# A list schedule's numbers, a port it now counts, and evictions over two chunks

## The chip, the cores and the metric

The kernel runs on one core of a Trainium2 chip: TensorE (PE, with its weight loads PEld), VectorE (DVE), ScalarE (ACT), GpSimd (POOL) and the DMA queue of SyncE (SP). The metric is the device time of one execution in microseconds, smaller is better. Before the change: median 906.44 us of 3 runs (905.68 to 906.60).

## The reference, cut to what matters

Windowed attention (4 batches, 8 heads, 576 positions, head size 64, each query sees itself and 63 keys before it), then two MLPs on the 2304 tokens of width 512, each with 2048 hidden units:

```python
scores = np.where(mask, scale * np.matmul(q, k.transpose(0, 1, 3, 2)), -1000000000.0)
attn = np.exp(scores - np.max(scores, axis=-1, keepdims=True))
attn = attn / (np.sum(attn, axis=-1, keepdims=True) + 1e-09)
x = np.matmul(attn, v)          # then laid out as 2304 tokens x 512
h = x @ w_in;  x = np.maximum(0.01 * h, h) @ w_out      # first MLP
h = x @ w_in2; out = (h * np.cos(h)) @ w_out2           # second MLP
```

## The kernel before, in words

**Arithmetic.** Matrix products of the MLPs are made in three passes: each operand is split into a high part and a low remainder (XH and XL for the activations, wh and wl for the weights, gh and gl for the hidden values), and high*high, high*low and low*high are summed in PSUM.

**Weights.** The host passes the weights as 64-bit words, 64 blocks of 512 KB. A block `u` goes through these operations: `wd` DMA into a staging tile `st`, `wv` and `ww` take the two 32-bit halves apart (ACT), `wb` three bit operations on DVE (L199, L200, L204: from `st` and `wa` to `wa` and `we`), `wm` and `wj` a product and a sum (L209, L213, POOL or DVE), `wh` rounds the high part (ACT), `wl` the remainder (L225, POOL or DVE).

**Attention.** 18 steps of 128 tokens. A step `i` has loads `lq`, `lv`; 32 score products `qk` (L278); per half of the heads `st` (mask L286 and row maximum L291, DVE), `ex` (4 exponentials, ACT), `re` (L303, L304, DVE), `no` (L308, POOL), `pt` (transposes L316, PE), `pe` (copy out of PSUM, L152 on ACT); then `pv` (32 products L328), `xh` (XH, ACT) and `xl` (XL, L337, DVE).

**MLPs.** Each layer is run in four phases of 4 chunks of 128 hidden units. In a phase the tokens go by in tiles; a chunk of a tile is a unit: `h` (12 products L420 to L422), `ca`, `mx`, `gh`, `gl` (split of the hidden values: ACT, DVE L430, ACT, DVE L435; in layer two a longer chain L458 to L468 and L442), and, two units behind, `o` (12 products L507 for 256 tokens) into accumulators `y`. After a tile's fourth chunk the accumulators are evicted: `ev`, L535 on DVE where a sum of earlier phases is added, a copy on ACT in a layer's first phase.

**What sets the order.** The first phase of layer one (9 tiles of 256 tokens, 36 units) runs together with the 18 attention steps and the first 16 weight blocks. Its order is made by `ListSchedule`: it places operations one by one, each on the engine where it would end first by a table of durations (`spared` is added for DVE where there is a choice), earliest due time (`s_due`, `w_due`, `u_due`) first among those that could start within `AT_ONCE`. What comes out is one fixed order for each engine; on the chip an engine runs its own list in that order and waits for data by semaphores only. After unit 38 a plain loop sets the order: `emit_H(i)`, `chain(i)`, `emit_O(i - 2)`, and then either all evictions that are waiting or, without any, pieces of weight work (`w_next`) and of the second layer's operand split (`x_next`). SP's DMAs are one queue in the order of the same list: a load that waits for a buffer holds those behind it.

Of the kernel before, what the change touches and what calls it, by code (L numbers as in the profile page):

```python
# [27 lines left out]
G = 4  # L28
# [3 lines left out]
TILES_FIRST = (256,) * 9  # L32
# [1 line left out]
TILES_LAST = (512, 512, 512, 512, 256)  # L34
T_SPLIT = 1536
SAME = dict(pe=0.0, dve=0.12, act=0.12, pool=0.05, dma=0.0, none=0.0)
AT_ONCE = 0.05
TILE_US, STEP_AHEAD = 18.0, 30.0
W_AHEAD, LATE_FROM, LATE_US = 22.0, 30.0, 8.0
SPARED_FIRST, SPARED = 0.3, 2.0  # L40
LAG = 2


class ListSchedule:
# [15 lines left out]
    def ready(self, name):  # L60
        ways, after, take, give, due, spared = self.ops[name]
        bufs = 0.0
        for x, p in enumerate(take):
            log, n = self.taken[p], self.pools[p] - take[:x].count(p)
            if len(log) >= n:
                t = self.given[p].get(log[-n])
                if t is None:
                    return None
                bufs = max(bufs, t + 0.2)
        if any(a not in self.done for a in after):  # L70
            return None
        best = None
        for engine, us, fn in ways:
            t = max(bufs, self.free.get(engine, 0.0))
            for a in after:
                t0, e0 = self.done[a]
                t = max(t, t0 + (SAME[engine] if e0 == engine else 0.35 if e0 == "pe" else 0.2))
            rank = t + us + (spared if engine == "dve" and len(ways) > 1 else 0.0)
            if best is None or rank < best[4]:
                best = (t, engine, us, fn, rank)  # L80
        return best

    def run(self):
        waiting = list(self.ops)
        while waiting:
            ready = [(name, r) for name in waiting if (r := self.ready(name)) is not None]
            assert ready, waiting[:40]
            now = min(r[0] for _, r in ready) + AT_ONCE
            name, (t, engine, us, fn, _) = min(
                (x for x in ready if x[1][0] <= now), key=lambda x: (self.ops[x[0]][4], x[1][0])  # L90
            )
            waiting.remove(name)
            take = self.ops[name][2]
            for x, p in enumerate(take):
                n = take[:x].count(p)
                self.taken[p].append((name, n) if n else name)
            fn(engine)
            end = self.free[engine] = t + us
            self.done[name] = (end + (1.1 if engine == "dma" else 0.0), engine)
            for p, taker in self.ops[name][3]:  # L100
                self.given[p][taker] = end
# [3 lines left out]
def attention_two_mlps(ctx, tc, q, k, v, w_in1, w_out1, w_in2, w_out2, out, seq):  # L105
# [164 lines left out]
    def a_scores(i, pool, tag):  # L270

        for hd in range(2):
            qk_t[i, hd] = pool.tile([P, NPR, P], F32, tag=tag, name=f"qk{i}_{hd}")
            S_t[i, hd] = sp.tile([P, NPR, P], F32, tag="S", name=f"S{i}_{hd}")
        for pr in range(NPR):
            for x in range(2):
                for hd in range(2):
                    nc.tensor.matmul(  # L278
                        qk_t[i, hd][halves[x], pr, :], qT[i][halves[hd], pr, halves[x]],
                        kT[i][halves[hd], pr, x * BLK:x * BLK + P], start=True, stop=True,  # L280
                    )
# [19 lines left out]
    def a_recip(i, heads):  # L301
        sums, inv = (sm_t[i][:, x, heads[0]:heads[-1] + 1, :] for x in (1, 2))
        nc.vector.tensor_scalar(out=inv, in0=sums, scalar1=1e-9, scalar2=None, op0=ALU.add)  # L303
        nc.vector.reciprocal(out=inv, in_=inv)  # L304
# [81 lines left out]
    work = []  # L386
# [12 lines left out]
    N = len(work)  # L399
    e_todo, x_todo = [], []  # L400

    def e_next(n, engine="act"):
        for _ in range(n):
            if e_todo:
                evac(*e_todo.pop(0), engine)
# [113 lines left out]
    def evac(w, d, y, engine="act"):  # L519
        l, p, t0, n = w["l"], w["p"], w["t0"], w["n"]  # L520
        if w["packed"]:
            b = t0 // P
            part, b = (YF[0], b) if t0 < T_SPLIT else (YF[1], b - T_SPLIT // P)
            dst = part[:, b:b + n // P, d:d + 2, :].rearrange("p b d t -> p d b t")
            y = y.rearrange("p (d b t) -> p d b t", d=2, t=P)
        elif l == 0:
            dst = yrange(t0, n, d)
            y = y.rearrange("p (b t) -> p b t", t=P)
        else:
            dst = yblock(t0 // P + d).rearrange("p k e -> p (k e)")  # L530
        sign = 1.0 if l == 0 else -1.0
        if p == 0:
            scaled(engine, dst, y, sign)
        else:
            nc.vector.tensor_tensor(out=dst, in0=dst, in1=y, op=ALU.add if l == 0 else ALU.subtract)  # L535
        if w["lastphase"]:
            if l == 0:
                x_todo.append((dst, d, t0, n))
            else:
                r0 = t0 + d * P  # L540
                nc.sync.dma_start(out=out[r0:r0 + P, :], in_=dst)
# [28 lines left out]
    n0 = len(TILES_FIRST) * G  # L570
# [8 lines left out]
            before[w_after[u]] = u  # L579

    def w_due(x):
        return x * TILE_US / 8 - W_AHEAD if x < 2 * G else LATE_FROM + LATE_US * (x - 2 * G)

    def add_w_dma(x):
        u = w_list[x]
# [6 lines left out]
    def ways(fn, **us):  # L592
        return [(e, t, fn) for e, t in us.items()]
# [14 lines left out]
        op("wl", ways(lambda e: w_lo(u, e), pool=1.24, dve=0.7), [f"wh{u}"], [], [("wa", f"wv{u}")])  # L608

    def s_due(i):  # L610
        return TILE_US / 2 * i - STEP_AHEAD

    def add_loads(i):
        ls.add(f"lq{i}", [("dma", 2.2, lambda e: qk_load(i))], [f"qk{i - 2}"] if i >= 2 else [], due=s_due(i) - 6.0)
# [2 lines left out]
    def add_attention(i):  # L617
        pool, tag = (ps_y, "y") if i < LEAD else (ps_a, "a")
        pairs = [f"{i}_{hd}" for hd in range(2)]
        prev = [f"{i - 1}_{hd}" for hd in range(2)]  # L620

        def op(kind, w, after, take=(), give=(), hd=None):
            name = f"{i}" if hd is None else pairs[hd]
            before = f"{i - 1}" if hd is None else prev[1] if hd == 0 else pairs[0]
            after = list(after) + ([kind + before] if kind + before in ls.ops else [])
            ls.add(kind + name, w, after, take, give, due=s_due(i), spared=SPARED)

        op("qk", ways(lambda e: a_scores(i, pool, tag), pe=1.1), [f"lq{i}"], [tag, tag, "S", "S"])
        for hd in range(2):
            taker = f"qk{i}" if hd == 0 else (f"qk{i}", 1)  # L630
            op("st", ways(lambda e, hd=hd: a_mask(i, hd), dve=1.32), [f"qk{i}"], give=[(tag, taker)], hd=hd)
            op("ex", ways(lambda e, hd=hd: a_exp(i, hd), act=1.62), ["st" + pairs[hd]], hd=hd)
        if i < LEAD:
            for hd in range(2):
                ls.add("re" + pairs[hd], ways(lambda e, hd=hd: a_recip(i, [hd]), dve=0.3), ["ex" + pairs[hd]], due=s_due(i))
        else:
            ls.add(f"re{i}", ways(lambda e: a_recip(i, [0, 1]), dve=0.32), ["ex" + pairs[1]], due=s_due(i))
        for hd in range(2):
            taker = f"qk{i}" if hd == 0 else (f"qk{i}", 1)
            op("no", ways(lambda e, hd=hd: a_norm(i, hd, e), pool=1.05, dve=0.75),  # L640
               ["re" + pairs[hd] if i < LEAD else f"re{i}"], hd=hd)
            op("pt", ways(lambda e, hd=hd: a_transpose(i, hd), pe=0.5), ["no" + pairs[hd]], ["a"], [("S", taker)], hd=hd)
            op("pe", ways(lambda e, hd=hd: a_transposed(i, hd, e), act=0.5, dve=0.66), ["pt" + pairs[hd]],
               ["PT"], [("a", "pt" + pairs[hd])], hd=hd)
        op("pv", ways(lambda e: a_values(i), pe=1.2), ["pe" + p for p in pairs] + [f"lv{i}"], ["a"],
           [("PT", "pe" + p) for p in pairs])
        op("xh", ways(lambda e: a_out(i, 0, e), act=0.5, dve=0.66), [f"pv{i}"])
        op("xl", ways(lambda e: a_out(i, 1, e), dve=0.62), [f"xh{i}"], give=[("a", f"pv{i}")])

    def u_due(i):  # L650
        return TILE_US * work[i]["ti"] + TILE_US / G * (i % G) + (TILE_US * len(TILES_FIRST) if i >= n0 else 0.0)

    def add_unit(i):
        w = work[i]
# [54 lines left out]
    for x in range(4 * G):  # L709
        add_weights(x)  # L710
    for i in range(n0 + LAG):
        add_unit(i)
# [6 lines left out]

    for i in range(n0 + LAG, N + LAG):  # L720
        if i < N:
            w_until(2 * work[i]["m"])
            emit_H(i)
        chain(i)
        w_until(2 * work[i - LAG]["m"] + 1)
        emit_O(i - LAG)
        if e_todo:
            e_next(len(e_todo))
        else:
            x_next(2)  # L730
            for _ in range(2 if i < N and work[i]["n"] == 512 else 1):
                w_next()
# [46 lines left out]
```

## Time and profile before

| | us |
|---|---|
| runs, median of 3 (lowest, highest) | 906.44 (905.68, 906.60) |
| profiled execution, its own time | 906.46 |
| its span in the profile | 904.7 |
| PE busy in the span | 868.3 (96%) |
| DVE, ACT, POOL busy | 599.8, 488.7, 294.7 |

The span runs from the first instruction to the last; 1.8 us of the execution's own time lie around it. Matmuls are pipelined: a matmul's duration overlaps the next one's, so counts of matmuls are turned into time by the pieces of the chain, which do not overlap. A busy PE at a granted clock of 1.00 of its full 2.4 GHz and one at half of that look alike; the clock column tells them apart.

### The profile page before, as it was taken

What the parts mean: (1) busy time and instruction counts of PE and PEld (TensorE: products, weight loads), DVE (VectorE), ACT (ScalarE), POOL (GpSimd) and SP (SyncE); (2) the same over time, 40 slices, a digit from 0 to 9 for tenths busy, and PEclk for the clock granted to TensorE, in tenths of its full rate; (3) what the DMA queues carried; (4) which work ended last, traced back from release to release, by engine and by line L of the source; (5) the groups of instructions that cost most, each with busy time, mean ns of one, the idle gap of its engine ahead of it and who ended that gap; (6) DMA issues with size and microseconds to landing.
All of it is one profiled execution on the core that took longest, in us unless ns stands there. A gap on an engine that the chain in (4) does not pass through costs nothing.

```text
span 904.7 us, 14203 instructions
## 1 busy us (share of the span) xinstructions
PE 868.3 (96%) x5424; PEld 743.5 (82%) x5424; DVE 599.8 (66%) x963; ACT 488.7 (54%) x1101; POOL 294.7 (33%) x257
## 2 busy tenths in 40 slices
PE   4489999999999999999999999999999999999998
PEld 3389999987888888988888888888888888788886
DVE  6997556566565555454785677767777777865565
ACT  6578677665433333424444567666555655544443
POOL 4545122156332133332566243322333233220000
PEclk9599999999999999999999999999999999999999
DMA  8456334112111011111111011101111011001111
GB/s 293 150 176 205 109 128 135 48 71 71 47 46 47 24 48 47 47 47 46 47 48 47 13 58 47 47 24 47 48 47 46 24 47 47 24 0 47 47 47 70
DMA packets 29092, 60.16 MB, mean 66 GB/s; under 512 B 2464, under 2 KB 11680, under 8 KB 29024
## 3 DMA queue, kind: packets, MB, share of 16 engines
q1 hardware_dynamic: 29024, 59.25, 19.1%
q8 instruction: 42, 0.69, 0.3%
q14 instruction: 26, 0.21, 0.1%
HBM read 54.53 MB, written 4.72 MB: 65 GB/s over the span
## 4 chain that ended last, share of the span: by engine, by line
PE 86%; DVE 8%; ACT 2%; issue 2%; DMA 1%; SPq 0%; POOL 0%; ACTq 0%; DVEq 0%; POOLq 0%
PE y L507 40%; PE h L420 14%; PE h L421 14%; PE h L422 14%; PE pv L328 2%; DVE wa L200 1%; PE pt L316 1%; DVE wa L199 1%; PE qk L278 1%; DMA qT<-in_q_dram 1%; DVE S L286 1%; DVE we L204 1%; DMA st<-in_moe_w_in_dram 1%; DVE YFa L535 1%; DVE sm L291 0%
## 5 line engine op out<-in xcount | busy, mean ns | idle before, releaser
L420 PE MATMUL h<-XH,wh 128*128 128x512 f32 (+1 forms) x704 | 250.9, 356 | 3.2 <-DVE ca L442 3.2
L421 PE MATMUL h<-XL,wh 128*128 128x512 f32 (+1 forms) x704 | 247.9, 352 | 0.9 <-DVE XL L337 0.9
L422 PE MATMUL h<-XH,wl 128*128 128x512 f32 (+1 forms) x704 | 247.5, 352 | 0.0
L420 PEld LDWEIGHTS h<-XH,wh 128*128 128x128 f32 x704 | 134.0, 190 | 24.3 <-DVE ca L442 4.6
L225 POOL TENSOR_TENSOR wl<-wa,wh 128x512 fp32r<-128x512 f32 x62 | 83.4, 1346 | 216.4 <-ACT wh L152 216.3
L421 PEld LDWEIGHTS h<-XL,wh 128*128 128x128 f32 x704 | 134.1, 190 | 18.9 <-DVE XL L337 1.2
L422 PEld LDWEIGHTS h<-XH,wl 128*128 128x128 f32 x704 | 134.0, 190 | 17.6
L435 DVE TENSOR_TENSOR gl<-ca,gh 128x512 fp32r<-128x512 f32 (+1 forms) x176 | 140.2, 797 | 9.4 <-ACT gh L152 9.4
L152 ACT ACTIVATE gh<-ca 128x512 fp32r<-128x512 f32 (+1 forms) x176 | 96.9, 551 | 89.0 <-PE y L507 61.4
L430 DVE TENSOR_TENSOR ca<-h,ca 128x256 f32<-128x256 f32 (+1 forms) x96 | 53.2, 554 | 131.2 <-ACT ca L152 131.0
L507 PE MATMUL y<-gh,wh 128*128 128x256 f32 (+1 forms) x384 | 131.2, 342 | 0.7 <-ACT gh L152 0.7
L507 PE MATMUL y<-gl,wh 128*128 128x256 f32 (+1 forms) x384 | 129.8, 338 | 1.7 <-DVE gl L435 1.6
L507 PE MATMUL y<-gh,wl 128*128 128x256 f32 (+1 forms) x384 | 129.0, 336 | 0.0
L209 POOL TENSOR_TENSOR wf<-wf,we 128x512 bf16<-128x512 bf16 x58 | 67.7, 1167 | 169.5 <-DVE we L204 164.5
L507 PE MATMUL y<-wh,gh 128*128 128x512 f32 x288 | 112.4, 390 | 0.3 <-ACT gh L152 0.3
L507 PE MATMUL y<-wl,gh 128*128 128x512 f32 x288 | 112.2, 390 | 0.0
L507 PE MATMUL y<-wh,gl 128*128 128x512 f32 x288 | 112.2, 389 | 0.0
L152 ACT ACTIVATE ca<-h 128x256 f32<-128x256 f32 (+1 forms) x96 | 46.7, 488 | 112.7 <-PE h L422 103.7
L460 DVE SCALAR_TENSOR_TENSOR cb<-ca,h 128x512 f32<-128x512 int32 (+1 forms) x80 | 50.6, 632 | 83.2 <-ACT ca L458 83.1
L467 ACT ACTIVATE cb<-ca 128x512 f32<-128x512 f32 (+1 forms) x80 | 47.2, 590 | 79.0 <-DVE ca L461 79.0
L458 ACT ACTIVATE ca<-h 128x512 int32<-128x512 f32 (+1 forms) x80 | 44.1, 552 | 79.5 <-PE h L422 78.4
L507 PEld LDWEIGHTS y<-gl,wh 128*128 128x128 f32 x384 | 72.8, 190 | 10.5 <-DVE gl L435 3.0
(58 smaller groups left out, 1284.8 us busy)
## 6 DMA issues: line engine op xcount, KB each, us to landing
st<-in_moe_w_in_dram SPq DMA_DIRECT2D x32, 512.0 KB, 3.5
st<-in_moe_w_out_dram SPq DMA_DIRECT2D x32, 512.0 KB, 3.5
v<-in_v_dram SPq DMA_DIRECT2D x35, 256.0 KB, 2.9
kT<-in_k_dram SPq DMA_DIRECT2D x17, 384.0 KB, 4.2
qT<-in_q_dram SPq DMA_DIRECT2D x18, 256.0 KB, 4.0
out_dram<-YFa SPq DMA_DIRECT2D x12, 256.0 KB, 2.2
out_dram<-YFb SPq DMA_DIRECT2D x6, 256.0 KB, 2.1
kT<-in_k_dram SPq DMA_DIRECT2D x1, 256.0 KB, 3.2
```

The source lines that it names most:

```text
L152: nc.scalar.activation(out=out_, in_=in_, func=AF.Copy, scale=scale)
L209: engines[engine].tensor_tensor(out=f, in0=f, in1=e, op=ALU.mult)
L225: engines[engine].tensor_tensor(out=wl, in0=mid.pop(u)[0], in1=wh.bitcast(F32), op=ALU.subtract)
L420: mm(h[:, :n], wh[:, 0, kk, :], xh, start=kk == 0, stop=False)
L421: mm(h[:, :n], wh[:, 0, kk, :], xl, start=False, stop=False)
L422: mm(h[:, :n], wl[:, 0, kk, :], xh, start=False, stop=kk == KD - 1)
L430: nc.vector.tensor_tensor(out=ca[i], in0=hps.pop(i)[:, :work[i]["n"]], in1=ca[i], op=ALU.max)
L435: nc.vector.tensor_tensor(out=gl[:, :n], in0=ca.pop(i), in1=gh[:, :n].bitcast(F32), op=ALU.subtract)
L458: nc.scalar.activation(out=kk, in_=h, func=AF.Copy, scale=INV2PI)
L460: nc.vector.scalar_tensor_tensor(out=b, in0=kk, scalar=-PI2_A, in1=h, op0=ALU.mult, op1=ALU.add)
L467: nc.scalar.activation(out=b, in_=a, func=AF.Sin, scale=0.5)
L507: mm(y, a, b, start=first and x == 0 and not (packed and d % 2), stop=last and x == 2, skip_group_check=packed)
```

## The change

Three things. First, `ListSchedule` keeps a second clock called `port`: POOL's operations, and DVE's operations whose names begin as `PORTED` lists them, are placed so that no two of them overlap in the list's own times. Second, the numbers that steer the list are others: due times of weights, steps and units, and the price `SPARED` of taking DVE where ACT or POOL could do it. `QK_AFTER` names step 18, and the steps are 0 to 17. Third, the loop after the first phase evicts two accumulators in a step instead of all that wait, and goes on with `x_next` and `w_next` in the step that takes the last of them.

```diff
-AT_ONCE = 0.05
-TILE_US, STEP_AHEAD = 18.0, 30.0
-W_AHEAD, LATE_FROM, LATE_US = 22.0, 30.0, 8.0
-SPARED_FIRST, SPARED = 0.3, 2.0
+AT_ONCE = 0.02
+TILE_US, STEP_AHEAD = 18.0, 38.54
+W_AHEAD, LATE_FROM, LATE_US = 23.97, 34.48, 6.89
+SPARED_FIRST, SPARED = 0.47, 0.55
+W_EACH, FIRST_STEPS, QK_AFTER, U_LATE = 3.04, 5.0, ('pt', 18, 1), -6.91
+PORTED = ("wv", "ww", "wb", "wm", "wj", "wh", "wl", "no", "gl")
...
+            if engine == "pool" or engine == "dve" and name[:2] in PORTED:
+                t = max(t, self.free.get("port", 0.0))
...
+            if engine == "pool" or engine == "dve" and name[:2] in PORTED:
+                self.free["port"] = end
...
-        return x * TILE_US / 8 - W_AHEAD if x < 2 * G else LATE_FROM + LATE_US * (x - 2 * G)
+        return x * W_EACH - W_AHEAD if x < 2 * G else LATE_FROM + LATE_US * (x - 2 * G)
...
-        return TILE_US / 2 * i - STEP_AHEAD
+        return TILE_US / 2 * i - (STEP_AHEAD if i > 1 else STEP_AHEAD + FIRST_STEPS)
...
-        return TILE_US * work[i]["ti"] + TILE_US / G * (i % G) + (TILE_US * len(TILES_FIRST) if i >= n0 else 0.0)
+        return TILE_US * work[i]["ti"] + TILE_US / G * (i % G) + U_LATE + (TILE_US * len(TILES_FIRST) if i >= n0 else 0.0)
...
-        if e_todo:
-            e_next(len(e_todo))
-        else:
+        more = len(e_todo) > 2
+        e_next(2 if i < N else len(e_todo))
+        if not more:
             x_next(2)
```

The same operations are issued as before, in another order and some on another engine. In the first phase these go from ACT to DVE: 6 of 38 `ca`, 5 of 38 `gh`, 6 of 36 `pe`, 3 of 18 `xh`, 1 of 18 `ev`; from POOL to DVE: 7 of 16 `wm`, and `wl` has one more there; from DVE to POOL: 2 `wj`; from DVE to ACT: 1 `ww`, 1 `wh`.

A step's loads are 384 KB of keys and 256 of queries and two times 256 of values, the first step's less (640 KB and 512 KB a step in all); a weight block has 512 KB.

SP's queue, from the first weight block on (before), and from the same place in the queue after the change (`kT` and `qT` are a step's keys and queries, `v` its values, `st` a weight block):

```order
L175 DMA st_187<-in_moe_w_in_dram 128x1024
L249 DMA kT_192<-in_k_dram 128x4x192
L254 DMA qT_194<-in_q_dram 128x512
L175 DMA st_202<-in_moe_w_in_dram 128x1024
L261 DMA v_233<-in_v_dram 128x512 x2
L175 DMA st_247<-in_moe_w_in_dram 128x1024
L249 DMA kT_258<-in_k_dram 128x4x192
L254 DMA qT_260<-in_q_dram 128x512
L175 DMA st_282<-in_moe_w_in_dram 128x1024
```

```order
L255 DMA kT_187<-in_k_dram 128x4x192
L260 DMA qT_189<-in_q_dram 128x512
L267 DMA v_194<-in_v_dram 128x512 x2
L181 DMA st_223<-in_moe_w_in_dram 128x1024
L255 DMA kT_235<-in_k_dram 128x4x192
L260 DMA qT_237<-in_q_dram 128x512
L181 DMA st_255<-in_moe_w_in_dram 128x1024
L255 DMA kT_286<-in_k_dram 128x4x192
L260 DMA qT_288<-in_q_dram 128x512
```

The second step's values move ahead of the first weight block, and a step's keys and queries stand ahead of each of the next weight blocks.

DVE's list before the second attention step's result `XL` (`S`, `sm`: scores and their maxima and sums; `wa`, `we`, `wf`: a weight block's parts; `PT`: transposed scores). Before, the first `XL` stands 26 rows ahead of the second, with three weight blocks' bit operations (L199, L200, L204) between them; the last 11 of these rows:

```order
L286 SCALAR_TENSOR_TENSOR S_0_362<-qk_0_361,m_112 128x512
L291 TENSOR_REDUCE sm_453<-S_0_362 128x4
L303 TENSOR_SCALAR sm_405<-sm_405 128x8
L304 RECIPROCAL sm_405<-sm_405 128x8
L154 CAST wh_293<-wa_387 128x512
L199 TENSOR_SCALAR wa_407<-wa_407 128x512
L200 SCALAR_TENSOR_TENSOR wa_407<-st_385,wa_407 128x512
L204 TENSOR_SCALAR we_483<-wa_407 128x512
L286 SCALAR_TENSOR_TENSOR S_1_364<-qk_1_363,m_112 128x512
L291 TENSOR_REDUCE sm_453<-S_1_364 128x4
L337 TENSOR_TENSOR XL<-pv_460,XH 128x4x128
```

After the change the whole stretch from the first `XL` to the second, eight rows further:

```order
L205 TENSOR_SCALAR wa_306<-wa_306 128x512
L206 SCALAR_TENSOR_TENSOR wa_306<-st_255,wa_306 128x512
L210 TENSOR_SCALAR we_392<-wa_306 128x512
L309 TENSOR_SCALAR sm_299<-sm_299 128x8
L310 RECIPROCAL sm_299<-sm_299 128x8
L215 TENSOR_TENSOR wf_327<-wf_327,we_392 128x512
L292 SCALAR_TENSOR_TENSOR S_1_343<-qk_1_342,m_112 128x512
L297 TENSOR_REDUCE sm_363<-S_1_343 128x4
L343 TENSOR_TENSOR XL<-pv_406,XH 128x4x128
```

Six weight blocks' bit operations stand ahead of the second `XL` before, two after.

DVE's list in layer two at the tile of 256 tokens (phase two), from `gl` through the evictions of the tile ahead of it (`YFa`) to the next `ca`, before:

```order
L435 TENSOR_TENSOR gl_6892<-ca_6843,gh_6891 128x256
L535 TENSOR_TENSOR YFa<-YFa,y_0_6758 128x512
L535 TENSOR_TENSOR YFa<-YFa,y_1_6762 128x512
L535 TENSOR_TENSOR YFa<-YFa,y_2_6766 128x512
L535 TENSOR_TENSOR YFa<-YFa,y_3_6770 128x512
L442 SCALAR_TENSOR_TENSOR ca_6888<-cb_6889,h_6874 128x256
L460 SCALAR_TENSOR_TENSOR cb_6930<-ca_6929,h_6915 128x256
```

And after:

```order
L441 TENSOR_TENSOR gl_6892<-ca_6843,gh_6891 128x256
L541 TENSOR_TENSOR YFa<-YFa,y_0_6756 128x512
L541 TENSOR_TENSOR YFa<-YFa,y_1_6760 128x512
L448 SCALAR_TENSOR_TENSOR ca_6888<-cb_6889,h_6874 128x256
L466 SCALAR_TENSOR_TENSOR cb_6928<-ca_6927,h_6913 128x256
L467 SCALAR_TENSOR_TENSOR ca_6927<-ca_6927,cb_6928 128x256
L441 TENSOR_TENSOR gl_6931<-ca_6888,gh_6930 128x256
L541 TENSOR_TENSOR YFa<-YFa,y_2_6764 128x512
L541 TENSOR_TENSOR YFa<-YFa,y_3_6768 128x512
L448 SCALAR_TENSOR_TENSOR ca_6927<-cb_6928,h_6913 128x256
```

Four evictions stood between one `gl` and the next `ca`; now there are two, and two more after the next chunk's operations.

## Rows read from the trace of the kernel before

**Rows 1.** The page: span, and shares of the chain that ended last.
```profile
span 904.7 us, 14203 instructions
...
PE 86%; DVE 8%; ACT 2%; issue 2%; DMA 1%; SPq 0%; POOL 0%; ACTq 0%; DVEq 0%; POOLq 0%
```

**Rows 2.** Windows: stretch, length; busy PE, PEld, DVE, ACT, POOL; clock, DMA, GB/s.
```profile
0.00:20.00 20.00, 8.95 (x116) 7.25 (x120) 12.80 (x24) 11.57 (x39) 10.30 (x26) 1.00 0.86 302
20.00:40.00 20.00, 8.71 (x104) 6.54 (x97) 19.48 (x29) 13.04 (x42) 13.19 (x11) 0.63 0.52 172
40.00:60.00 20.00, 16.00 (x168) 14.79 (x169) 19.53 (x32) 12.99 (x39) 7.96 (x7) 0.77 0.44 142
60.00:80.00 20.00, 19.64 (x261) 18.19 (x262) 18.26 (x34) 16.39 (x61) 10.87 (x10) 1.00 0.68 228
80.00:180.00 100.00, 100.00 (x1319) 95.07 (x1314) 57.90 (x119) 72.82 (x261) 23.93 (x24) 1.00 0.35 112
180.00:220.00 40.00, 37.62 (x271) 33.48 (x270) 29.09 (x39) 24.77 (x50) 24.61 (x20) 1.00 0.20 69
220.00:905.00 685.00, 677.41 (x3206) 568.15 (x3204) 442.75 (x690) 337.16 (x615) 203.81 (x164) 1.00 0.12 43
```

**Rows 3.** Timeline: start, us, engine, line, operation, count [idle before and releaser].
```profile
7.21 0.69 DVE L286 SCALAR_TENSOR_TENSOR S<-qk,m 128x512 f32<-128x512 f32 x1 [5.55 <-PE qk L278]
...
42.02 0.68 DVE L337 TENSOR_TENSOR XL<-pv,XH 128x512 fp32r<-128x512 f32 x1
...
42.75 0.58 PE L421 MATMUL h<-XL,wh 128*128 128x256 f32 x1 [0.87 <-DVE XL L337]
...
51.33 0.43 DVE L204 TENSOR_SCALAR we<-wa 128x512 uint16<-128x512 uint16 x1
```

**Rows 4.** Single lines, 0 to 215 us: shortest, median, longest ns; first, last start; forms.
```profile
L199 DVE TENSOR_SCALAR wa<-wa x16: 417/1258/1546, 10.9 to 207.7; 128x512 uint32<-128x512 uint32 x16
...
L200 DVE SCALAR_TENSOR_TENSOR wa<-st,wa x16: 691/693/1647, 12.2 to 209.2; 128x512 uint32<-128x512 uint32 x16
...
L204 DVE TENSOR_SCALAR we<-wa x16: 426/427/1339, 13.0 to 210.9; 128x512 uint16<-128x512 uint16 x16
...
L303 DVE TENSOR_SCALAR sm<-sm x19: 160/170/1265, 10.3 to 178.1; 128x8 f32<-128x8 f32 x17, 128x4 f32<-128x4 f32 x2
...
L286 DVE SCALAR_TENSOR_TENSOR S<-qk,m x36: 650/682/692, 7.2 to 174.6; 128x512 f32<-128x512 f32 x36
...
L337 DVE TENSOR_TENSOR XL<-pv,XH x18: 637/691/694, 22.2 to 184.5; 128x512 fp32r<-128x512 f32 x18
...
L430 DVE TENSOR_TENSOR ca<-h,ca x38: 372/423/681, 52.6 to 214.3; 128x256 f32<-128x256 f32 x36, 128x512 f32<-128x512 f32 x2
...
L435 DVE TENSOR_TENSOR gl<-ca,gh x37: 373/426/1818, 53.5 to 212.6; 128x256 fp32r<-128x256 f32 x36, 128x512 fp32r<-128x512 f32 x1
```

**Rows 5.** Chain that ended last, 60 to 97 us: start, us, what.
```profile
59.54 5.04 DMA st<-in_moe_w_in_dram
...
65.91 1.54 ACT S L296 x8
...
81.56 0.44 PE pt L316 x4
...
82.36 1.03 PE qk L278 x32
...
85.04 1.08 PE pv L328 x32
...
93.57 1.43 PE y L507 x12
```

**Rows 6.** Waits of ACT to 90 us: us in total, times, longest.
```profile
ACT wa L152 <- DMA st<-in_moe_w_in_dram: 1.6, 1, 1.6
```

**Rows 7.** Waits, 186 to 222 us.
```profile
PE y L507 <- DVE gl L435: 1.6, 4, 0.5
```

**Rows 8.** Timeline at the 256-token tiles of the last layer's middle phases.
```profile
671.38 2.47 DVE L535 TENSOR_TENSOR YFa<-YFa,y 128x512 f32<-128x512 f32 x4
...
674.24 0.38 PE L420 MATMUL h<-XH,wh 128*128 128x256 f32 x1 [1.44 <-DVE ca L442]
...
774.23 0.39 PE L420 MATMUL h<-XH,wh 128*128 128x256 f32 x1 [1.41 <-DVE ca L442]
```

More of the change, by code (lines that the diff above doesn't have):

```diff
@@ L626, in op @@
             ls.add(kind + name, w, after, take, give, due=s_due(i), spared=SPARED)
-        op("qk", ways(lambda e: a_scores(i, pool, tag), pe=1.1), [f"lq{i}"], [tag, tag, "S", "S"])
+        op("qk", ways(lambda e: a_scores(i, pool, tag), pe=1.1), [f"lq{i}"] + ([QK_AFTER[0] + f"{i - QK_AFTER[1]}_{QK_AFTER[2]}"] if i >= max(QK_AFTER[1], 2) else []), [tag, tag, "S", "S"])
         for hd in range(2):
```

## The prediction, as it was put on record

> **What bounds the kernel now.** Read first the page's chain and then the windows. The chain that ended last runs through PE for 86% of the span of 904.7 us [rows 1]. The windows [rows 2] say where PE is not the bound: from 220 us to the end it lacks 7.3 us of 684.7, from 80 to 180 nothing, from 180 to 220 2.4 us, and before 80 us it is busy for only 53.3 of 80, much of it at a lower clock (granted 0.63 and 0.77 between 20 and 60 us, so partly at 1.2 GHz instead of 2.4). So nearly all that a new order can give lies in the first 80 us, and there DVE is busy for 57.3 of the 60 us from 20 to 80: it is DVE's list that hands PE its work.
>
> To measure this I use one number, PE's debt: the time at which an instruction starts, less the full-speed work that stands ahead of it in PE's list. The pieces of the chain [rows 5] give that work: 32 score products 1.03 us, 4 transposes 0.44, 32 value products 1.08, 12 products of a unit 1.43 (a quarter, which is how the list moves them, 0.36). The chain's piece at 85.04 is the seventh group of value products; ahead of it in PE's list stand 9 score groups, 14 of transposes, 6 of values and 59 quarters: 9.3 + 6.2 + 6.5 + 21.1 = 43.0 us. The debt is 42.0 us there, and from then on PE is full.
>
> What makes DVE slow is read from single lines [rows 4]. The bit operations of a weight block take 0.42, 0.69 and 0.43 us at best, and up to 1.55, 1.65 and 1.34; the median of the first is 1.26. The mask, which reads PSUM, never leaves 0.65 to 0.69. From DVE's first score work at 7.21 to the end of the eighth block's bits at 51.76 [rows 3], DVE's list holds 8 score pairs at 1.37 (0.68 for the mask, as much for the maximum), 8 blocks at 1.54, and 20 smaller operations worth 9.8: 33.1 us at best durations. It took 44.6. The 11.5 us are slip, most of it such stretched instructions.
>
> The Trainium skill, "SBUF — State Buffer", section "Who interferes with whom", says that VectorE and GpSimd share a pair of SBUF ports as an exclusive lock: a VectorE operation with two SBUF inputs, or one like tensor_scalar in a two-port mode, and a GpSimd operation block each other whole. The rows agree on who is stretched. By the same rule the small L303, and the hidden values' copies that move to DVE, take the lock as well, and the changed list does not count them; if each of the 11 L303 ahead of the deciding point were stretched like the longest of them (1.27 against 0.17 [rows 4]), the debt would grow by 12 us. The trace says less: the median of 19 is the short one, so only a few are caught.
>
> **The change, part by part.** *First phase (the large term).* In the new DVE list six things stand otherwise: weight bits come later, attention steps sooner. Up to the second step's XL DVE's list holds 18.3 us of work at best durations instead of 27.5; that XL ended at 42.70 and the first unit's second product waited for it [rows 3]. So units start far sooner; but they also need weights, and DVE's list gets longer before PE is full: it takes copies and splits from ACT and products from POOL. The point that decides is where the debt is largest. I went down the PE list at each output group of the first two tiles: the largest comes at the output of unit 7, which needs that unit's gl. DVE's list up to it: 22 score pairs (30.1), 9 weight blocks (13.9), 8 XL at 0.69 as the mask's row (5.5), 9 mx and 8 gl at 0.43 (7.3), 11 re at 0.36 (4.0: L303's 0.17 and as much for its second half), 7 products of weights at the third bit line's 0.43 and 4 sums and remainders at the second's 0.69 (5.8), and 9 operations that the trace does not show on DVE or shows once (4.8: PSUM copies of 512 at the mask's 0.69, of 256 at gl's 0.43). That is 71.4; instructions start a few hundredths before the one ahead ends, so I take 70. On top come waits: the steps now follow each other so closely that DVE waits for scores and exponentials, 0 to 8, I take 4. And what is left of the slip: at least 0, at most the old one by weight blocks, 11.5 x 9/8 = 13; the lists place lock users apart, but an engine's list binds only itself, so they will meet when either is late; I take a third, 4. So gl of unit 7 ends at 7.2 + 70 + 4 + 4 = 85.2. PE's list ahead of that output: 11 score groups, 18 of transposes, 8 of values, 65 quarters: 11.3 + 7.9 + 8.6 + 23.2 = 51.1. Debt 34.1 instead of 42.0: **-8**. Ends: no slip and no wait 77.2, debt 26.1, -16; all of the old slip 94.2, debt 43.1, +1.
>
> ACT gives work away but must run 19 of the exponentials' groups at 1.54 [rows 5] before the last weight of the first four chunks, 56.8 us of list from 8.7: done at 65.5, while DVE wants it at about 75. It is covered, with 9 us to spare. SP's loads: the first weight block now stands behind 1.14 MB more (the second step's 640 and 512 KB); at 302 GB/s [rows 2] that is 3.8 us later, and ACT wants it only after two groups of exponentials, which it now does first. QK_AFTER names a step that does not exist: nothing.
>
> *End of the first phase.* From 180 to 220 us PE lacks 2.4 us, 1.6 of it waiting for gl behind weight bits [rows 2, 7]. In the new list two or three blocks' bits still stand between one gl and the next, but their products move to DVE at 0.43 and POOL's list behind the last attention step falls from 18 operations to 12. **-1**, from -2.4 to +2 (ACT's next split stands behind a weight that is loaded only after DVE's bits).
>
> *Evictions.* In layer two's middle phases PE waits 1.44 and 1.41 us at the tile of 256 tokens, for a ca that stands behind four evictions of 2.47 us in all [rows 8]. With two, that ca starts 1.2 us sooner; the other two go behind the next chunk, where DVE has four operations at 0.43 and these 1.2 us in a chunk whose products take PE 1.43 and about as much again. Behind the postponed pair waits the next tile's third and fourth accumulator only in name: six buffers rotate, and these two take the ones evicted first. **-2**, from -2.9 to 0. The other tiles have 512 tokens and twice the room.
>
> Sum: -8 - 1 - 2 = -11 on a span of 904.7: 893.7, and with the 1.76 us around it 895.5. The profiled execution's own 906.46 is the median's 906.44 but for 0.02.
>
> **Rivals.** *The locks stay* (0.15). For it: an order on each engine cannot keep two engines apart, and both lists are nearly full. Against: the list leaves POOL idle where DVE has its bits. First phase +1, the rest -3: 904.6 us. *Nothing is left of them* (0.13): DVE runs at best durations with 2 us of waits, first phase -14, evictions -2.5, end of the phase -1.5: 888.5. *ACT stalls behind weight loads* (0.07), the slower one. Weights stand in SP's queue behind loads that wait for PE, and ACT takes them in order, with exponentials behind. For it: such a load is 5.04 us of the chain at 59.5 [rows 5]. Against: ACT waited 1.6 us for them in all up to 90 us [rows 6]. Nine blocks at 3 us each are 27: the weights are done at 93 instead of 75, unit 7's output 10 later, debt 52, +10 less 3: 913.5. It decides from 2.3 us a block on.
>
> **How the numbers follow.** The forecast has 0.65 and its own range is 890 to 901. From 887 to 905 holds it, the better case and half of the first rival. A measurement of this kernel tells about 0.2% from no change (904.6 to 908.3). Faster: 0.65 + 0.13 + a part of the first rival, 0.83; same 0.09; slower 0.08.
>
> **What would show it.** In the profile after: the first three bit lines with medians near 0.42, 0.69 and 0.43; the first unit's products some 10 us before 42; unit 7's output near 85 with PE full behind it; PE lacking under 17 us instead of 26.7 in the first 80; waits at the 256-token tiles under 0.5. The forecast is wrong if DVE's bits keep their 1.26, if ACT's waits for weight loads pass 10 us, or if PE is full early and gives the time back between 180 and 220.

## The result, and the profile after

The changed kernel takes 897.0 us (median of 4 runs, 896.12 to 897.41) and the kernel before 906.47 (905.68 to 906.6): ratio 0.9898, 95% interval 0.9885 to 0.991, so 9.5 us faster. The forecast was 895.5 with 887 to 905 around it. The profiled execution spans 894.9 us against 904.7. The page's first line, and of its part 4 the shares by engine of the chain that ended last, answer to [rows 1]:

```profile
span 894.9 us, 14169 instructions
...
PE 84%; DVE 8%; ACT 4%; DMA 2%; issue 1%; POOL 1%; SPq 0%; DVEq 0%; ACTq 0%; POOLq 0%
```

The windows, in the columns of [rows 2]:

```profile
0.00:20.00 20.00, 10.67 (x152) 8.75 (x156) 10.85 (x24) 11.46 (x43) 9.78 (x26) 1.00 0.77 258
20.00:40.00 20.00, 16.23 (x243) 13.74 (x236) 18.16 (x36) 17.90 (x63) 11.75 (x12) 0.91 0.77 276
40.00:60.00 20.00, 15.96 (x213) 14.33 (x207) 19.30 (x38) 16.96 (x63) 10.00 (x10) 0.91 0.58 180
60.00:80.00 20.00, 18.37 (x260) 16.48 (x257) 17.86 (x37) 18.31 (x66) 11.81 (x11) 1.00 0.75 254
80.00:180.00 100.00, 99.25 (x1201) 94.67 (x1200) 64.64 (x131) 62.79 (x204) 24.92 (x22) 1.00 0.29 87
180.00:220.00 40.00, 38.40 (x220) 33.45 (x220) 24.86 (x43) 21.95 (x42) 16.38 (x13) 1.00 0.25 82
```

Between 20 and 40 us PE is busy for 16.23 us instead of 8.71, at a granted clock of 0.91 instead of 0.63; DVE is hardly less busy. Before 80 us PE lacks 18.8 us instead of 26.7. The timeline, as in [rows 3], has the second step's XL at 26.84 instead of 42.02, and the gl of unit 7, on which the forecast's largest term rested:

```profile
26.84 0.68 DVE L343 TENSOR_TENSOR XL<-pv,XH 128x512 fp32r<-128x512 f32 x1
...
29.77 0.41 PE L427 MATMUL h<-XL,wh 128*128 128x256 f32 x1
...
82.33 0.41 DVE L441 TENSOR_TENSOR gl<-ca,gh 128x256 fp32r<-128x256 f32 x1
```

Of the single lines of [rows 4] (0 to 215 us; shortest, median, longest ns), the first bit line's median fell from 1258 ns to 420, though some of its instructions are still stretched:

```profile
L205 DVE TENSOR_SCALAR wa<-wa x17: 417/420/1352, 14.7 to 205.9; 128x512 uint32<-128x512 uint32 x17
...
L206 DVE SCALAR_TENSOR_TENSOR wa<-st,wa x17: 691/692/1411, 15.2 to 206.4; 128x512 uint32<-128x512 uint32 x17
...
L210 DVE TENSOR_SCALAR we<-wa x17: 426/428/1406, 15.9 to 207.1; 128x512 uint16<-128x512 uint16 x17
...
L309 DVE TENSOR_SCALAR sm<-sm x19: 160/166/1032, 10.4 to 165.0; 128x8 f32<-128x8 f32 x17, 128x4 f32<-128x4 f32 x2
```

One number compares all kernels below. I call it PE's loss: for every matmul, the time to the next one's start less that form's interval at full speed (0.227 us with 512 columns, 0.120 with 256, the pieces of [rows 5] shared out over their matmuls for the others), with the 5 us before the first matmul counted in. It holds waits and products at the lower clock alike. Summed, it is the span less the same work, some 847.1 us, in every run. All values are us. Of the stretches three are shown, the last of them where the eviction edit acts; the others hold 0.5 and 4.7 to 5.0 in every run.

| kernel | 0 to 180 | 180 to 230 | 640 to 800 | span | median |
|---|---|---|---|---|---|
| before | 44.8 | 4.2 | 3.3 | 904.7 | 906.47 |
| changed | 36.0 | 2.6 | 4.0 | 894.9 | 897.0 |
| changed, old evictions | 36.4 | 2.6 | 3.3 | 894.6 | 896.46 |
| before, new evictions | 44.8 | 4.2 | 4.0 | 905.4 | 906.88 |
| changed, no port clock | 40.4 | 7.3 | 4.3 | 904.6 | 906.1 |
| before, port clock alone | 39.4 | 21.8 | 3.3 | 916.8 | 920.61 |
| the same, STEP_AHEAD new | 44.4 | 21.4 | 3.3 | 921.4 | 923.02 |
| the same, SPARED pair new | 38.5 | 6.4 | 3.3 | 900.7 | 902.54 |
| the same, both new | 38.6 | 1.1 | 3.3 | 895.4 | 897.39 |
| changed, SPARED pair old | 39.4 | 6.4 | 4.0 | 902.1 | 905.53 |
| changed, third eviction loop | 37.2 | 2.6 | 1.0 | 893.0 | 894.1 |
| both new, third eviction loop | 37.3 | 1.5 | 1.0 | 892.2 | 896.46 |

(Some medians stand further above the span plus 1.8 us than others: the profiled execution is one of the runs, and a kernel's runs scatter by up to 3.7 us. For the port clock alone, the changed kernel with the old SPARED pair and the last row it was the fastest run, 1.7 to 2.5 us below the median. The loss scatters too: the kernels whose first phase has one and the same order lost 36.0, 36.4 and 37.2 us before 180, or 38.6 and 37.3, so a difference of some 1.3 us in that column tells nothing.)

### The profile page after: what moved, and what is told of

It is laid out like the page before. It is cut to its first block, busy times and chain, and to the rows that moved or that the text cites. A ratio compares the mean times of both kernels' runs of the same rounds, so it can differ in the third digit from the quotient of the medians.

```text
span 894.9 us, 14169 instructions
## 1 busy us (share of the span) xinstructions
PE 866.9 (97%) x5424; PEld 740.9 (83%) x5424; DVE 596.9 (67%) x988; ACT 481.6 (54%) x1082; POOL 288.2 (32%) x251
## 4 chain that ended last, share of the span: by engine, by line
PE 84%; DVE 8%; ACT 4%; DMA 2%; issue 1%; POOL 1%; SPq 0%; DVEq 0%; ACTq 0%; POOLq 0%
PE y L513 40%; PE h L426 14%; PE h L427 13%; PE h L428 13%; PE qk L284 2%; DVE wa L206 1%; PE pv L334 1%; ACT S L302 1%; PE pt L322 1%; DVE we L210 1%; DVE gl L441 1%; DMA st<-in_moe_w_in_dram 1%; DVE wa L205 1%; DVE YFb L541 1%; DMA st<-in_moe_w_out_dram 1%
## 5 line engine op out<-in xcount | busy, mean ns | idle before, releaser
L441 DVE TENSOR_TENSOR gl<-ca,gh 128x512 fp32r<-128x512 f32 (+1 forms) x176 | 142.5, 810 | 5.6 <-ACT gh L158 5.5
L158 ACT ACTIVATE gh<-ca 128x512 fp32r<-128x512 f32 (+1 forms) x171 | 94.8, 554 | 89.4 <-PE y L513 59.9
L231 POOL TENSOR_TENSOR wl<-wa,wh 128x512 fp32r<-128x512 f32 x61 | 80.5, 1321 | 189.2 <-ACT wh L158 189.2
L215 POOL TENSOR_TENSOR wf<-wf,we 128x512 bf16<-128x512 bf16 x51 | 60.3, 1182 | 182.1 <-DVE we L210 182.1
L158 ACT ACTIVATE ca<-h 128x512 f32<-128x512 f32 (+1 forms) x90 | 44.7, 496 | 122.4 <-PE h L428 109.1
L219 POOL TENSOR_TENSOR wa<-wa,wf 128x512 f32<-128x512 f32 x62 | 80.2, 1294 | 29.5 <-DVE wf L215 17.8
```

The source lines that it names most:

```text
L158: nc.scalar.activation(out=out_, in_=in_, func=AF.Copy, scale=scale)
L215: engines[engine].tensor_tensor(out=f, in0=f, in1=e, op=ALU.mult)
L219: engines[engine].tensor_tensor(out=a, in0=a, in1=f, op=ALU.add)
L231: engines[engine].tensor_tensor(out=wl, in0=mid.pop(u)[0], in1=wh.bitcast(F32), op=ALU.subtract)
L441: nc.vector.tensor_tensor(out=gl[:, :n], in0=ca.pop(i), in1=gh[:, :n].bitcast(F32), op=ALU.subtract)
```

## The experiments

### The port clock and the numbers, one without the other

Out of the changed kernel the port clock was taken, in both places where it stands, and all the new numbers were kept:

```
-            if engine == "pool" or engine == "dve" and name[:2] in PORTED:
+            if False:
                 t = max(t, self.free.get("port", 0.0))
...
-            if engine == "pool" or engine == "dve" and name[:2] in PORTED:
+            if False:
                 self.free["port"] = end
```

> The changed kernel without the port clock, its numbers and evictions kept. Theory (the port clock makes the gain): DVE's list alone is no longer (its largest debt at best durations 25 us against 27), but the first bit line's median rises from 0.42 towards 1.26 and 6 to 8 us come back: 903 to 905. Rival (the new due times make the gain): the time stays within 1 us of 897.

Measured: 906.1 us (905.7 to 906.91), ratio to before 1.0 (0.9991 to 1.0008). Without the port clock nothing is left of the gain, and more came back than the theory's 903 to 905. The sign that the theory named did not come: the first bit line's median stays near 0.42.

```profile
L205 DVE TENSOR_SCALAR wa<-wa x17: 414/427/1517, 14.5 to 215.0; 128x512 uint32<-128x512 uint32 x17
```

A median does not tell how many instructions are stretched as long as it is less than half of them; the sum does. The groups by line, DVE, 0 to 90 us (instructions | busy us, mean ns | idle before), show what the clock does. The kernel before:

```profile
L200 DVE SCALAR_TENSOR_TENSOR wa<-st,wa 128x512 uint32<-128x512 uint32 x11 | 11.3, 1027 | 0.4
L199 DVE TENSOR_SCALAR wa<-wa 128x512 uint32<-128x512 uint32 x11 | 9.6, 871 | 0.0
L204 DVE TENSOR_SCALAR we<-wa 128x512 uint16<-128x512 uint16 x11 | 6.2, 563 | 0.6
```

The changed kernel:

```profile
L206 DVE SCALAR_TENSOR_TENSOR wa<-st,wa 128x512 uint32<-128x512 uint32 x11 | 9.0, 822 | 0.4
L205 DVE TENSOR_SCALAR wa<-wa 128x512 uint32<-128x512 uint32 x11 | 6.1, 557 | 0.0
L210 DVE TENSOR_SCALAR we<-wa 128x512 uint16<-128x512 uint16 x11 | 5.4, 493 | 0.5
```

The changed kernel without the clock:

```profile
L206 DVE SCALAR_TENSOR_TENSOR wa<-st,wa 128x512 uint32<-128x512 uint32 x11 | 10.0, 909 | 0.4
L205 DVE TENSOR_SCALAR wa<-wa 128x512 uint32<-128x512 uint32 x11 | 9.7, 883 | 0.0
L210 DVE TENSOR_SCALAR we<-wa 128x512 uint16<-128x512 uint16 x11 | 7.2, 658 | 0.6
```

Eleven blocks at the best 1.54 us would be 16.9. The kernel before takes 27.1, the changed one 20.5, and the one without the clock 26.9: the numbers alone unstretch next to nothing. They still lower PE's loss before 180 us by 4.4 (the steps stand elsewhere in the order; what of that does it was not tried), but lose 3.1 of it again between 180 and 230 and 1.0 at the evictions.

The other way round, the kernel before got the port clock and kept its numbers:

```
+            if engine == "pool" or engine == "dve" and name[:2] in PORTED:
+                t = max(t, self.free.get("port", 0.0))
...
+            if engine == "pool" or engine == "dve" and name[:2] in PORTED:
+                self.free["port"] = end
```

> The kernel before with the port clock alone, old numbers and old evictions. Theory (the port clock makes the gain): the bit lines' medians fall to 0.42, 0.69, 0.43 and most of the gain is there, 897 to 899. Rival (the numbers make it): 904 to 907.

Measured: 920.61 us (918.56 to 921.12), ratio 1.0155. Both theories missed, by 13.6 us and more. The first phase did what was expected (39.4 instead of 44.8; the three bit lines take 19.4 us), and all of it and more went between 180 and 230. The waits of PE from 180 to 220 us name the place:

```profile
PE y L513 <- DVE gl L441: 15.2, 2, 15.0
```

and the timeline of that stretch the cause (columns as in [rows 3]):

```profile
187.50 0.42 ACT L158 ACTIVATE gh<-ca 128x256 fp32r<-128x256 f32 x1 [1.25 <-PE y L513]
...
191.65 1.15 POOL L215 TENSOR_TENSOR wf<-wf,we 128x512 bf16<-128x512 bf16 x1
...
192.83 0.43 DVE L210 TENSOR_SCALAR we<-wa 128x512 uint16<-128x512 uint16 x1 [2.26 <-POOL wf L215]
192.87 1.39 POOL L219 TENSOR_TENSOR wa<-wa,wf 128x512 f32<-128x512 f32 x1
193.17 1.38 DVE L205 TENSOR_SCALAR wa<-wa 128x512 uint32<-128x512 uint32 x1
...
195.00 1.39 POOL L231 TENSOR_TENSOR wl<-wa,wh 128x512 fp32r<-128x512 f32 x1 [0.74 <-ACT wh L158]
196.35 1.15 POOL L215 TENSOR_TENSOR wf<-wf,we 128x512 bf16<-128x512 bf16 x1
...
197.54 0.43 DVE L210 TENSOR_SCALAR we<-wa 128x512 uint16<-128x512 uint16 x1 [2.27 <-POOL wf L215]
...
202.59 1.71 DVE L441 TENSOR_TENSOR gl<-ca,gh 128x256 fp32r<-128x256 f32 x2
...
204.02 0.58 PE L513 MATMUL y<-gl,wh 128*128 128x256 f32 x1 [15.00 <-DVE gl L441]
```

Read it from the bottom. PE waits 15 us for a gl at 202.59. On DVE's row four blocks' bits stand ahead of it, and the last of each, L210, waits for POOL's product L215 of the block before, for `we` has one buffer. POOL does all three of a block's products and sums (L215, L219, L231), and a block goes round every 4.71 us (192.83 to 197.54). Its own input, gh, was done at 187.92. This order is the list's doing. Why it comes out so is read from the code and not measured: a block is due before any unit, POOL's operations and DVE's bits now hold the same clock, and whenever it comes free a weight takes it.

### Which number the port clock needs

Ten numbers of the change have an effect: the SPARED pair, STEP_AHEAD and seven others (QK_AFTER names no step). Three kernels take the one above and change some of them, one takes the pair out of the changed kernel. First the surcharge on DVE (SPARED), which decides whether a block's product goes to POOL:

```
-SPARED_FIRST, SPARED = 0.3, 2.0
+SPARED_FIRST, SPARED = 0.47, 0.55
```

> The kernel before with the port clock, old evictions, and one number pair of the change: SPARED_FIRST, SPARED = 0.47, 0.55; the due times stay old. Without that pair the same kernel took 920.6 us, with PE standing 15.2 us at 188.7 for gl, which stood on DVE's row behind four weight blocks, while POOL did three additions and multiplications of each in a chain of 4.7 us a block. Theory A (a surcharge of 2.0 us on DVE sends wm, wj and wl all to POOL, and under the port clock POOL's chain shuts gl out; with 0.55 wm goes to DVE and gl gets turns): the jam goes, 901 us (897 to 906). Rival B (the jam comes because attention ends too late, at 178.9 instead of 171.7, so only STEP_AHEAD mends it): 919 us or more.

Measured: 902.54 us (901.43 to 902.65), ratio 0.9956 (0.9941 to 0.9971). Then the attention steps' due times alone:

```
-TILE_US, STEP_AHEAD = 18.0, 30.0
+TILE_US, STEP_AHEAD = 18.0, 38.54
```

> The kernel before with the port clock, old evictions, and only STEP_AHEAD = 38.54 of the change's numbers (SPARED stays 2.0). Theory A: the stretch 180 to 220 keeps its loss of over 15 us, 919 us (914 to 924). Rival B (attention further ahead is what mends it): 901 us (897 to 906).

Measured: 923.02 us (922.36 to 924.08). PE's waits from 180 to 230 us, with the surcharge's pair new:

```profile
PE y L513 <- DVE gl L441: 3.9, 2, 3.2
```

and with STEP_AHEAD new instead:

```profile
PE y L513 <- DVE gl L441: 14.8, 1, 14.8
```

The surcharge is what jams; B falls twice.

The second kernel shows something else as well. Its three bit lines take 17.7 us to 90 us, less than the 19.4 with the clock alone, and yet PE's loss before 180 is back at 44.4. DVE was busy for only 15.36 us between 40 and 60, where it was for 18.81 with the clock alone; and up to 180 PE waited 5.9 us for POOL's S (L314) instead of 3.1, and 4.4 for ca instead of 0.3. So unstretched bit lines alone do not make the gain; which of these waits comes first was not followed up.

Both edits together:

> The kernel before with the port clock, old evictions, SPARED_FIRST, SPARED = 0.47, 0.55 and STEP_AHEAD = 38.54. Theory A with the dates of attention as a second, smaller need (close some 7 us earlier than with SPARED alone): 898 us (895 to 901), within 3 us of the changed kernel without the remaining five numbers. Rival C (all the numbers are needed together): over 903 us.

Measured: 897.39 us (897.18 to 898.14), ratio 0.9904 (0.9889 to 0.9918), with no wait of PE over the view's floor between 180 and 230 us. The timeline of DVE there shows the other order:

```profile
188.40 0.43 DVE L210 TENSOR_SCALAR we<-wa 128x512 uint16<-128x512 uint16 x1
188.93 1.50 DVE L215 TENSOR_TENSOR wf<-wf,we 128x512 bf16<-128x512 bf16 x1
190.35 0.41 DVE L441 TENSOR_TENSOR gl<-ca,gh 128x256 fp32r<-128x256 f32 x1
...
192.83 0.43 DVE L210 TENSOR_SCALAR we<-wa 128x512 uint16<-128x512 uint16 x1
193.37 0.42 DVE L215 TENSOR_TENSOR wf<-wf,we 128x512 bf16<-128x512 bf16 x1
193.71 1.51 DVE L441 TENSOR_TENSOR gl<-ca,gh 128x256 fp32r<-128x256 f32 x1
```

The product L215 runs on DVE, so L210 waits for nobody, and a gl follows every block. That some of them are stretched (1.50, 1.51 us) no longer reaches PE. STEP_AHEAD beside it gives 5.3 us, all between 180 and 230 (6.4 to 1.1); with the old surcharge it cost 5.0 in the first phase. The other seven numbers together are not to be told from nothing: 896.46 with them and the old evictions, 897.39 without, and the intervals of the two ratios overlap. The last of the four:

> The changed kernel with SPARED_FIRST, SPARED = 0.3, 2.0 as before. Theory A: POOL's chain is longer again, but the earlier due times keep gl of four units ahead of the blocks, so no jam of 15 us and a loss of some 5 us between 180 and 220: 902 us (899 to 907). Rival D (the surcharge alone decides, whatever the due times): 915 us or more. Rival B (the due times alone decide): 897 us.

Measured: 905.53 us (903.87 to 907.54), ratio 0.9997 (0.9987 to 1.0006). A's mechanism and range hold, its number was 3.5 low: there is no 15 us jam, but 3.8 us more between 180 and 230, and 3.4 more before 180, which I had not counted (both from the profiled run, the fastest of ten). Neither D nor B stands: surcharge and due times both matter.

### The evictions

The changed kernel with the old loop:

```
-        more = len(e_todo) > 2
-        e_next(2 if i < N else len(e_todo))
-        if not more:
+        if e_todo:
+            e_next(len(e_todo))
+        else:
```

> The changed kernel with the old eviction loop (all that wait in one step). Theory: the split evictions won nothing, since the 1.4 us that PE waits at the 256-token tile came back as 1.36 us in the next tile, where two evictions now share a step with a weight block's bits; so 896.5 (0.5 us under the changed kernel), with PE waits of 1.4 at the 256-token tiles and none after them. Rival (the prediction's term): the split is worth 2 us, 899.

Measured: 896.46 us (894.26 to 896.71). And the opposite, the kernel before with the new loop alone:

> The kernel before with the changed eviction loop alone. Theory (the loop mends the stall of the 256-token tile and lets sums and a weight block into the chunk of the full tile's accumulators, where the same time is lost): 906.9 us (906 to 908). Rival (what was predicted for this edit: 2 us less): 904.4 us.

Measured: 906.88 us (905.78 to 907.53), ratio 1.0007 (0.9998 to 1.0016). From both sides the edit is worth nothing that the times can show, as both theories had it. Its trace in the changed kernel: at the 256-token tile there are two evictions ahead of ca, and hardly a stall; 15 us on, at the full tile behind, the loss of [rows 8] is back. The timeline (DVE, POOL, and the PE row that waits):

```profile
660.95 1.27 DVE L541 TENSOR_TENSOR YFa<-YFa,y 128x512 f32<-128x512 f32 x2
...
662.14 0.41 DVE L448 SCALAR_TENSOR_TENSOR ca<-cb,h 128x256 f32<-128x256 f32 x1
...
675.99 1.27 DVE L541 TENSOR_TENSOR YFb<-YFb,y 128x512 f32<-128x512 f32 x2
...
677.19 0.41 DVE L205 TENSOR_SCALAR wa<-wa 128x512 uint32<-128x512 uint32 x1
...
677.40 1.35 POOL L231 TENSOR_TENSOR wl<-wa,wh 128x512 fp32r<-128x512 f32 x1 [2.48 <-ACT wh L158]
...
677.64 1.67 DVE L206 SCALAR_TENSOR_TENSOR wa<-st,wa 128x512 uint32<-128x512 uint32 x1
...
679.41 0.43 DVE L210 TENSOR_SCALAR we<-wa 128x512 uint16<-128x512 uint16 x1
679.75 0.68 DVE L448 SCALAR_TENSOR_TENSOR ca<-cb,h 128x512 f32<-128x512 f32 x1
...
680.49 0.50 PE L426 MATMUL h<-XH,wh 128*128 128x512 f32 x1 [1.20 <-DVE ca L448]
```

In the old loop a chunk with evictions took no weight block. The new test asks only whether more than two were waiting, so the full tile's chunk, which has just two, now does its two evictions and a block's bits, 0.98 us of them stretched against POOL's L231; ca comes 1.20 us late. If that is the cause, a loop that lets nothing else into any chunk with fresh accumulators keeps the one gain without the other loss:

```
+        waiting = len(e_todo)
         emit_O(i - LAG)
-        more = len(e_todo) > 2
+        fresh = len(e_todo) > waiting
         e_next(2 if i < N else len(e_todo))
-        if not more:
+        if not fresh:
```

> The changed kernel, evictions still two in a step, but weight pieces and operand splits left out in every step in which new accumulators became ready, as before. Theory (weight bits in the step of the two evictions of the 256-token tile make the new wait of 1.36 us): both of these waits go, and the old ones of 1.4 stay away: 3 us less, 894. Rival (the wait comes from the evictions being spread at all): 896.5 to 897.5.

Measured: 894.1 us (893.16 to 894.88), ratio to before 0.9863 (0.9848 to 0.9878), as the theory had it and faster than the changed kernel, whose interval lies above. PE's loss from 640 to 800 us falls from 4.0 to 1.0, and at the full tile ca now follows the evictions at once:

```profile
677.07 1.27 DVE L541 TENSOR_TENSOR YFb<-YFb,y 128x512 f32<-128x512 f32 x2
...
678.26 0.68 DVE L448 SCALAR_TENSOR_TENSOR ca<-cb,h 128x512 f32<-128x512 f32 x1
...
680.21 0.39 PE L426 MATMUL h<-XH,wh 128*128 128x512 f32 x1
```

Last, the SPARED pair, STEP_AHEAD, the port clock and this loop on the kernel before:

> The kernel before with the port clock, only two of the change's numbers (SPARED_FIRST, SPARED = 0.47, 0.55 and STEP_AHEAD = 38.54), and evictions spread two to a chunk without sums and weight blocks in any chunk in which a new accumulator came ready. Theory (the parts add up): 897.4 us with the old evictions, less the 2.3 us of stalls at the two 256-token tiles: 895.1 us (894 to 896.5). Rival (at the two tiles the weight blocks that were put off come due later and stall there): 897 us or more.

Measured: 896.46 us (894.0 to 897.08), ratio 0.9896 (0.9881 to 0.9912). The stalls are gone in its profile (1.0 from 640 to 800, span 892.2), but that execution was the fastest of four, and the median lies at the upper edge of the theory's range, half a microsecond under the rival's. The parts add up in the trace; the time alone doesn't settle it. Best of all measured is the changed kernel with the third loop.

## Why the prediction was right, and where it was not

**First phase, right in size (-8, measured -8.8).** With the numbers held, the port clock takes stretch and loss away together: the bit lines lose 6.4 us and PE's loss before 180 falls by 4.4 from the kernel without the clock to the changed one; it is 7.7 and 5.4 from the kernel before to the clock alone. The clock also changes the order, and no run parts that from the stretch. That DVE's list is what feeds PE is borne out in part: STEP_AHEAD alone shows that little stretch is not enough.

The terms fit less well than their sum. The gl of unit 7 ended at 82.74, forecast 85.2. From 7.31 to there DVE's instructions took 74.3 us by their own times, 2.9 more than the forecast's list of 71.4 (slip, forecast 4); DVE stood idle for 7.3 (waits, forecast 4); and they overlapped their neighbours by 6.1, for which the forecast had taken off 1.4. Nor was this the point that decides. PE's debt at the first product that reads this gl, at 83.33, was some 32 us instead of 34.1, and it was the same already at unit 5's, at 79.30: PE did not wait for it. And PE was not full behind it; it lost 4.0 us between 90 and 180, where before it lost 3.0. So some 10 us were won by then and over 1 was given back: that -8.8 lies so near -8 is partly luck. In the first 80 us PE lacked 18.8 and not under 17.

What the forecast did not see is that the clock and the numbers are one edit: either half gains 4.4 or 5.4 us before 180 and gives it back, or more, at 180 to 230.

**The little operations.** The Trainium skill, "SBUF — State Buffer", section "Who interferes with whom", has `tensor_scalar` among the operations that can take the pair of ports that DVE and GpSimd share. By that the small L309 takes the lock too, which I had put at +12 us if all were caught. The trace agrees for some of them: from 0 to 90 us 12 of them take 4.1 us, where 12 at their median of 0.17 are 2.0.

```profile
L309 DVE TENSOR_SCALAR sm<-sm 128x8 f32<-128x8 f32 (+1 forms) x12 | 4.1, 338 | 1.0 <-ACT S L302 1.0
```

Four were caught, and it cost 2.1 us; but the ten of the kernel before had taken 3.6 instead of 1.7, so the change lost next to nothing by it. Of the hidden values' copies, for which I had said the same, it holds for one kind only. The five from SBUF (gh, L160) have a median of 294 ns, and two of them took 603 and 1000 beside an operation of POOL's; the six that read PSUM (ca, L162) took 411 to 425, two of them beside one.

**End of the first phase, right (-1, measured -1.6).** The reason that it gave, products that move to DVE, is the one that the SPARED pair bears out: beside the port clock it takes PE's loss there from 21.8 to 6.4. But the price was argued from the waits of before, with +2 as the worst, and the due times, worth 5.3 there, were not in it. The port clock under the old surcharge shows what can stand there: 17.6 us more. A loss between 180 and 220 was among the signs of being wrong, but no rival of mine had its place there, where the sign of this change was decided.

**Evictions, wrong (-2, measured +0.7 in PE's loss).** The 256-token tiles did what was said: 0.2 us lost at each instead of 1.6. The step that failed is the sentence "The other tiles have 512 tokens and twice the room". They have the room, but the edit's new condition fills it with a weight block that the old one kept out, and the same 1.4 us is lost there, twice.

**The rivals.** The locks did not stay, but they are not all gone: of the 10.2 us that the bit lines took to 90 us beyond their best 16.9, 3.6 are left. ACT's waits for weight loads up to 90 us, as in [rows 6], were four, the longest 1.1 us, under the 2.3 at which that rival decides:

```profile
ACT wa L158 <- DMA st<-in_moe_w_in_dram: 2.2, 3, 0.8
ACT wa L158 <- DMA st<-in_moe_w_out_dram: 1.1, 1, 1.1
```

The sum: -8.8 - 1.6 + 0.7 is -9.7 of the span's -9.8. Against the forecast's -11 the evictions gave 2.7 too little and the other two terms 1.4 more than their size. That QK_AFTER does nothing was not tried; by the code its condition, `i >= 18`, holds for none of the steps 0 to 17.

## What to carry to other kernels

If a scheduler learns that two engines exclude each other, look at its old prices in the same step: here a surcharge that pushed work to the helper engine was harmless while the two clocks were free, and under a common clock it let the weights shut out a late operation of 0.4 us for 15. Judge stretched instructions by their sum, not by their median, and do not take less stretch for a gain: one kernel here had almost none in its bit lines and was the slowest. When a condition in a loop is rewritten, list every case in which the new one answers differently, not only the case it was written for. And compare kernels by the bottleneck engine's loss per stretch: medians that agreed (906.1 and 906.47) hid a gain of 4.4 us and a loss of about as much.

## What the runs showed of the hardware

Some DVE operations that start just behind one of POOL's end only behind it. In the timeline of the port clock alone, L219 on POOL ran from 192.87 to 194.26, and L205 on DVE, 0.42 us by its median, from 193.17 to 194.55; POOL's own L219 took 1.39 there and 1.23 at 186.93. An operation of 128x8 elements is held as well: in the changed kernel one L309, 166 ns by the median, ran from 53.08 to 54.11 beside POOL's L314 from 53.04 to 54.08. Others were never held there: the mask, which reads PSUM, stayed within 639 to 692 ns over its 36 and the row maximum (L297), a reduction, within 685 to 689, though 16 of each started while POOL had an operation running.
